# Expert 0's first window of rows moved into the attention's plan, expert 2's weight loads ordered behind transposes, and filler products in later gaps of TensorE

## The chip, the cores and the metric

The kernel runs on one core of one Trainium2 chip. The metric is the device time of one execution in microseconds (us). PE is TensorE, DVE is VectorE, ACT is ScalarE, POOL is GpSimd and SP is SyncE, whose only work here is to issue DMAs.

## The reference

Three stages follow one another, all in float32.

```
# 1. attention: 4 x 8 heads, 768 steps, head width 48
k_n = k / (norm(k) + 1e-06)
for t in range(S):
    y[:, :, t] = einsum('bhd,bhde->bhe', q[:, :, t], state)
    v_old = einsum('bhde,bhd->bhe', state, kt)
    state = state + bt * einsum('bhd,bhe->bhde', kt, vt - v_old)
x = y as 3072 rows of 384

# 2. routed layer: 8 experts, 384 -> 1024 -> 384; each row goes to the expert of its largest logit
e_idx = argmax(x @ w_gate)
h = max(x[mask] @ w1[e], 0); ye = h @ w2[e]
out[mask] = gate_w[mask] * eom[mask, e] * ye

# 3. dense layer: 4 experts, 384 -> 1024 -> 384, all rows through all of them
p = domain_probs / (sum(domain_probs) + 1e-09)
out += p[:, e] * (max(x @ w1[e], 0) @ w2[e])
```

Which rows an expert of stage 2 gets is known only from the attention's output.

## The kernel before

Each stage builds a `Plan` (L103): a list of operations with an engine, an assumed cost, what each reads and writes, and a priority (a lower number goes first). `order` (L130) schedules the list once, before the program is built, and the program then holds every engine's instructions in that fixed order. Nothing is reordered on the chip: an instruction that waits holds up everything behind it on its engine, and a DMA that waits holds up everything behind it on its queue.

**Attention.** The 768 steps go in 12 chunks of 64, each a chain of small matmuls with evacuations by ACT and DVE between them (`rw`, `Sp` and `pb` are its PSUM banks). As soon as a tile of 128 rows of output is there, `Router.done` transposes it (L529), copies it with ACT (`xT`), and multiplies it with the gate weights (L536), and `place` (L540 on) works out where each row goes (L554, L570). The last chunk's rows come out at the end, so that the last stretch is one chain: output, transpose, gate product, place, list of rows (`wid`, L615). Where the plan has a gap of more than 300 ns on PE, it puts `fill` in (L249): a 128 x 128 product on a tile of zeros into a bank's unused part, between `FROM` and `FEND` of planned time.

**Routed layer, `moe1`.** Weights are in two float16 parts (high and low, cast by ACT L738 and DVE L739), so are the rows (`xh`) and the hidden values (`h`), and each product takes three matmuls. An expert's rows are gathered by POOL (`xg<-xd,wid`, L774), normalised and split (DVE L578 to L583, ACT L581), transposed by a DMA of the SP queue (`xt<-xh`) and put through `window_` (L779): 72 matmuls with the first weight (L787), whose 8 results are evacuated by ACT (L789) and DVE (L790), and 72 with the second (L799), whose 3 results are evacuated by L801 and L802 and written to DRAM by the POOL queue (`x<-y`, L805). An expert has 432 rows at most in the fixed program. The first 192 rows of experts 0 and 1 are taken out of the first 16 tiles, gathered during the attention and transposed into `xe` (`early`, L584), and the weights of these two experts are cast during the attention (into `kq`, `wa` and `wb`). So experts 0 and 1 have an early window of 192 rows (`xe`) and a second one of 240 (`xt`); the others have one of 432. Weights of expert 2 go into `w`, those of expert 3 into `kq` again, those of expert 4 into `wa`. Weights pass through three staging tiles `s0` to `s2`.

The tiles of `moe1` are taken from the memory that the attention's tiles held; the framework adds the waits which that needs.

**Dense layer, `moe2`.** It reads the DRAM tiles `x2` block by block (L928, L947).

Of the kernel before, what the change touches and what calls it, by code (L numbers as in the profile page):

```python
# [17 lines left out]
N, DM, NE, FF, NE2 = 3072, 384, 8, 1024, 4  # L18
# [5 lines left out]
WIN = 432  # L24
# [65 lines left out]
TRI = 450  # L90
UP = 1070
PW = 1080
FEND = 100000
FIN = 6
GRP = (6, 6, 4, 6, 2)

# [386 lines left out]
class Router:  # L483

    NXR=4
    def __init__(self,ctx,tc,dp):
        self.tc=tc; self.nc=tc.nc; self.xd=dp.tile([N,XW],F32,name="xd"); self.eld=dp.tile([N+512,MW],F32,name="eld"); self.ord=dp.tile([NE*N+512,1],I32,name="ord")
        c=self.c=ctx.enter_context(tc.tile_pool(name="rc",bufs=1)); T=lambda n,s,d=F32: c.tile(s,d,name=n)
        self.wgo=T("wgo",[128,KD,16])
        self.tri=T("tri",[128,128],F16); self.ones16=T("ones16",[128,128],F16)  # L490
        self.desc=T("desc",[128,8])
        self.row=T("row",[128,NT,MW]); self.LG,self.pr,self.tok=self.row[:,:,0:16],self.row[:,:,16:20],self.row[:,:,20]; self.acc,self.wid=T("acc",[128,NE,4]),T("wid",[128,NE,4],U32); self.OH=T("OH",[128,NT,8],F16)
        self.M2,self.MX=(T(n,[128,NT]) for n in ("M2","MX")); self.RK=T("RK",[128,NT],I32); self.EL=T("EL",[128,4,4,MW]); self.am,self.sc=T("am",[128,4]),T("sc",[128,4])
        self.run=T("run",[128,8],F16); self.kq=T("kq",[128,2*KD*FF*2],F16); self.wa,self.wb=(T(n,[128,2*KD*FF],F16) for n in ("wa","wb")); self.cnt=T("cnt",[128,8])
        self.xe=[T(f"xe{e}",[128,2*KD,EW],F16) for e in range(2)]; self.few=T("few",[128,8])
# [215 lines left out]
class Moe:  # L711
# [3 lines left out]
    def __init__(self,ctx,tc,r,w1,w2,v1,v2,out):  # L715
        self.ctx=ctx; self.tc=tc; self.nc=tc.nc; self.r=r; self.w=(w1,w2); self.v=(v1,v2); self.out=out
        p=ctx.enter_context(tc.tile_pool(name="vw",bufs=1)); self.dp=ctx.enter_context(tc.tile_pool(name="mdp",bufs=1,space=DRAM))
        r.c=ctx.enter_context(tc.tile_pool(name="fin",bufs=1))
        n=2*KD*FF; self.kq=[r.kq[:,0:n],r.kq[:,n:]]
        self.vw=[[p.tile([128,2,KD,FF],F16,name=f"v1{e}") for e in range(2)],[p.tile([128,2,4,7,192],F16,name="v20")]]  # L720

        a=[t.bitcast(F32).rearrange("p (j d) -> p j d",d=DM) for t in (r.kq,r.wa)]; self.acc=lambda j: a[j//16][:,j%16]
        w=r.wb; self.xk=[[w[:,1024*(KD*i+k):1024*(KD*i+k)+1024].rearrange("p (y t) -> p y t",y=2) for k in range(KD)] for i in range(2)]
        self.x2=[self.dp.tile([128,2,N+WIN],F16,name=f"x2{k}") for k in range(KD)]
        pp=ctx.enter_context(tc.tile_pool(name="pp",bufs=1,space=PSUM)); self.bank=[pp.tile([128,512],F32,name=f"b{i}") for i in range(8)]
    gate=(); slow=1.0
    def op(self,e,dur,fn,reads=(),writes=(),**k):
        k.setdefault('prio',self.prio); self.pl.add(e,dur,fn,reads,writes,**k)
    def dma(self,out,in_,reads,writes,xfer,turn=False):
# [12 lines left out]
    def weight(self,t,key,src,n,width):  # L742

        t=t.rearrange("p (l n f) -> p l n f",l=2,n=n); step=1024//width
        v=src.rearrange("(n p) f -> p n f",p=128); self.claim(key)
        for a in range(0,n,step):
            m=step*width; s,k=self.stage(m)
            self.dma(s.rearrange("p (n f) -> p n f",f=width),v[:,a:a+step],(),[k],m*WX)
            h,l=(t[:,j,a:a+step].rearrange("p n f -> p (n f)") for j in range(2))
            for x in range(0,m,m//2): self.pair(s[:,x:x+m//2],h[:,x:x+m//2],l[:,x:x+m//2],[k,key],key+(a,x))  # L750
        out=[key+(a,x,j) for a in range(0,n,step) for x in (0,m//2) for j in (0,1)]; self.parts.setdefault(key,set()).update(out); return out
# [94 lines left out]
    def moe1(self):  # L846
        nc=self.nc; tc=self.tc; r=self.r; pl=self.pl=Plan(tc,HOP); self.si=self.xi=self.bi=self.ci=self.hi=self.yi=0; self.pp_=0; self.parts={}
        with ExitStack() as c:
# [7 lines left out]
            def fetch(e):  # L856
                if e>=NE: return
                i=B_[e]; self.prio=10*(e-1)-3; x=self.gather(wid[:,e],e,0 if e>1 else EW); self.prio=10*(e-2)+3 if e>2 else 2
                t=[t.rearrange("p (l n f) -> p l n f",l=2,n=n) for t,n in zip(W[i],(KD,KF))]
                kw=[self.weight(W[i][j],('W',i,j),self.w[j][e],n,f) for j,n,f in ((0,KD,FF),(1,KF,DM))] if e>1 else [[('W',i,0)],[('W',i,1)]]  # L860
                ahead[e]=x,t,kw
            def colf(e):
# [8 lines left out]
            for e in range(NE):  # L871
                x,t,kw=ahead.pop(e); self.prio=10*e+5
                for m in range(6):
                    if e==4: self.weight6(self.vw[0][0],('v',0,0),self.v[0][0],m)
                    if e==5 and m<4: self.weight7(self.vw[1][0],('v',0,1),self.v[1][0],m)
                    if e==6: self.weight6(self.vw[0][1],('v',1,0),self.v[0][1],m)
                if e==0:
                    colf(1); cols[0][0]=0; x1,t1,kw1=ahead[1]
                    self.pp_=0; self.window_(0,*t,kw,(r.xe[0],[]),cols[0]); self.pp_=3; late=self.window_(1,*t1,kw1,(r.xe[1],[]),cols[1],ys=ye)
                    self.pp_=6; put(0); self.window_(0,*t,kw,x,cols[0],EW); self.prio=10  # L880
                    for f in late: f()
                else:
# [105 lines left out]
def deltanet_moe(tc,q,k,v,beta,wg,wo,w1,w2,probs,v1,v2,out):  # L988
    nc=tc.nc
    with ExitStack() as ctx:  # L990
        dp=ctx.enter_context(tc.tile_pool(name="dp",bufs=1,space=DRAM))
        r=Router(ctx,tc,dp)
        with ExitStack() as c2:
            plan=Plan(tc,HOP)
            at=Attention(c2,tc,plan,q,k,v,beta,r.wa,r.wb,r.done)
            at.prio=0
            at.ahead=r.weights; r.setup(c2,at,plan,wg,wo,probs); r.ahead=(w1,w2); at.run(); r.counts()
            plan.emit()
        m=Moe(ctx,tc,r,w1,w2,v1,v2,out)
        m.moe1(); m.moe2()  # L1000
# [28 lines left out]
```

## Time and profile before

| | |
|---|---|
| runs (us) | 1251.54, 1254.93, 1254.89, median 1254.89 |
| profiled execution (us) | 1257.36 |
| its span (us) | 1255.8 |
| PE busy | 1179.4 us, 94% of the span |
| DVE, ACT, POOL busy | 62%, 49%, 51% |
| mean granted PE clock | 0.965 |

The profile covers one execution, and its times are counted from the span's start. The granted clock is 1.00 where PE runs at its higher level (2.4 GHz) all the time and 0.50 where it runs at the lower one (1.2 GHz). The attention ends at 311 us, the routed layer at 538 us, and the rest is the dense layer.

### The profile page before, as it was taken

Reading aid. Unit: us, or ns where it says so; the run is one execution under the profiler, and the core shown is the slowest. Engines: PE = TensorE matmul, PEld = TensorE weight load, DVE = VectorE, ACT = ScalarE, POOL = GpSimd, SP = SyncE. Lnnn points to the kernel's source line nnn. Section 1 sums busy time; section 2 is a strip of 40 time slices with the busy share of each in tenths; the row PEclk is TensorE's granted clock in tenths of the full one; section 3 lists DMA queues with packets and bytes.
Section 4 is the critical chain, followed back from the end, with each engine's and each line's share of the span. In section 5 each row is a group of like instructions: output and inputs, shape, how many; then the busy total and the mean of one; then the engine's idle time right before and its main releaser. Section 6 shows DMA issues by size and latency. Waiting matters only on the chain.

```text
span 1255.8 us, 38782 instructions
## 1 busy us (share of the span) xinstructions
PE 1179.4 (94%) x16595; PEld 1031.4 (82%) x16595; DVE 781.1 (62%) x1583; ACT 618.7 (49%) x1129; POOL 640.4 (51%) x896
## 2 busy tenths in 40 slices
PE   6988888877989999999999999999999999999997
PEld 5877777766974555589999999999999999999997
DVE  3766837664777787236666566677565776555555
ACT  4546664543545655235445444454444454444442
POOL 9643431442474350055665454576444675566565
PEclk9889998886999999999999999999999999999999
DMA  8445442324779976021111111111111220111101
GB/s 137 84 94 121 97 98 45 98 74 110 182 176 233 244 184 175 29 67 39 40 39 39 35 43 44 48 51 39 34 44 50 65 64 28 37 54 52 52 27 39
DMA packets 151457, 100.74 MB, mean 80 GB/s; under 512 B 107696, under 2 KB 140432, under 8 KB 151280
## 3 DMA queue, kind: packets, MB, share of 16 engines
q1 hardware_dynamic: 133520, 69.18, 22.4%
q0 software_dynamic: 9216, 23.50, 6.7%
q10 hardware_dynamic: 8544, 5.53, 1.5%
q8 instruction: 131, 2.15, 0.7%
q14 instruction: 46, 0.38, 0.1%
HBM read 77.09 MB, written 15.77 MB: 74 GB/s over the span
## 4 chain that ended last, share of the span: by engine, by line
PE 56%; DVE 0%; issue 0%; POOL 0%; ACT 0%; POOLq 0%
PE b L928 30%; PE b L947 26%; POOL out_dram L966 0%; DVE h L940 0%; DVE cc L958 0%; DVE wa L962 0%; DVE sm L958 0%; ACT h L939 0%; ACT a L930 0%; POOL sep L965 0%; POOLq L1024 0%; POOLq L966 0%
## 5 line engine op out<-in xcount | busy, mean ns | idle before, releaser
L928 PE MATMUL b<-wb,v 128*128 128x256 f16 x3456 | 392.6, 273 | 0.4 <-PEq L895 0.4
L928 PEld LDWEIGHTS <-v 128*128 128x128 f16 x3456 | 336.7, 98 | 37.8 <-issue 0.8
L947 PE MATMUL b<-v,h 128*128 128x192 f16 x4032 | 348.2, 246 | 0.0
L947 PEld LDWEIGHTS <-h 128*128 128x128 f16 x4032 | 335.5, 98 | 2.4 <-DVE h L940 0.2
L936 POOL TENSOR_TENSOR S<-a 128x256 f32<-128x256 f32 x192 | 150.8, 804 | 249.8 <-ACT a L930 249.5
L940 DVE TENSOR_TENSOR h<-a,h 128x768 f16<-128x768 f32 x96 | 132.6, 1381 | 134.8 <-ACT h L939 126.5
L940 DVE TENSOR_TENSOR h<-S,h 128x1024 f16<-128x1024 f32 x96 | 117.7, 1226 | 125.8 <-ACT h L939 125.6
L930 ACT ACTIVATE a<-b 128x512 f32<-128x512 f32 x192 | 113.8, 595 | 151.2 <-PE b L928 149.1
L939 ACT ACTIVATE h<-S 128x1024 f16<-128x1024 f32 x96 | 101.4, 1056 | 161.7 <-POOL S L936 142.1
L936 POOL TENSOR_TENSOR S<-S,a 128x256 f32<-128x256 f32 x96 | 126.9, 1322 | 0.0
L939 ACT ACTIVATE h<-a 128x768 f16<-128x768 f32 x96 | 80.9, 843 | 3.0
L936 POOL TENSOR_TENSOR S<-a,S 128x256 f32<-128x256 f32 x96 | 77.0, 802 | 7.2
L958 DVE TENSOR_TENSOR cc<-b,sm 128x192 f32<-128x192 f32 x192 | 58.5, 345 | 2.4 <-ACT sm L952 2.4
L789 ACT ACTIVATE h<-b 128x432 f16<-128x432 f32 (+2 forms) x80 | 35.7, 454 | 40.3 <-PE b L787 36.3
L805 POOL DMA_DIRECT2D x<-y x27 | 19.3, 721 | 68.9 <-DVE y L802 60.8
L790 DVE SCALAR_TENSOR_TENSOR h<-b,h 128x432 f16<-128x432 f32 (+2 forms) x80 | 40.7, 511 | 17.5 <-ACT h L789 17.1
L774 POOL DMA_INDIRECT xg<-xd,wid x28 | 30.2, 1077 | 38.7 <-DVE xh L583 22.0
L958 DVE TENSOR_TENSOR sm<-b,sm 128x192 f32<-128x192 f32 x144 | 46.2, 348 | 1.5
L799 PE MATMUL b<-h,kq 128*128 128x432 f16 (+2 forms) x288 | 42.4, 304 | 4.8 <-DVE h L790 4.8
L787 PE MATMUL b<-xt,w 128*128 128x432 f16 x216 | 42.1, 355 | 2.5 <-DVE wa L739 2.0
L739 DVE SCALAR_TENSOR_TENSOR v<-s,v 128x512 f16<-128x512 f32 (+2 forms) x56 | 41.6, 761 | 4.1 <-ACT v L738 3.9
L267 POOL DMA_DIRECT2D stw<-in_moe_w_dram x28 | 16.0, 571 | 52.6 <-DVE X L374 19.9
(279 smaller groups left out, 1748.0 us busy)
## 6 DMA issues: line engine op xcount, KB each, us to landing
wb<-x SPq DMA_DIRECT2D x72, 256.0 KB, 3.2
s<-in_moe_w_dram SPq DMA_DIRECT2D x40, 384.0 KB, 4.2
s<-in_moe_w_dram SPq DMA_DIRECT2D x18, 512.0 KB, 4.3
s<-in_moe_w_dram SPq DMA_DIRECT2D x24, 256.0 KB, 4.7
xd<-ys ACTq DMA_DIRECT2D x24, 192.0 KB, 3.1
x<-y POOLq DMA_DIRECT2D x18, 216.0 KB, 4.2
stw<-in_moe_w_dram POOLq DMA_DIRECT2D x12, 256.0 KB, 4.0
stw<-in_moe_w_dram POOLq DMA_DIRECT2D x16, 192.0 KB, 3.5
```

The costliest lines, as they stand in the source:

```text
L739: self.op('V',(150+1.042*n)*self.slow,lambda: self.nc.vector.scalar_tensor_tensor(out=lo,in0=s,scalar=64.0,in1=hi,op0=ALU.mult,op1=ALU.sub ...
L787: nc.tensor.matmul(out=ps,lhsT=w1[:,a,k,f*128:(f+1)*128],rhs=xt[:,b*KD+k],start=i==0,stop=i==8); i+=1
L789: self.op('A',160+.85*n,lambda ps=ps,h=h: nc.scalar.activation(out=h[:,0],in_=ps,func=AF.Relu),[('p1',pi)],[('h',hi,0)],**U)
L790: self.op('V',150+1.042*n,lambda ps=ps,h=h: nc.vector.scalar_tensor_tensor(out=h[:,1],in0=ps,scalar=0.0,in1=h[:,0],op0=ALU.max,op1=ALU.sub ...
L799: nc.tensor.matmul(out=ps,lhsT=w2[:,a,f,d*128:(d+1)*128],rhs=hs[f][0][:,b],start=(f,i)==(0,0),stop=(f,i)==(KF-1,2))
L928: for c,y in PASS: nc.tensor.matmul(out=F[k][:,f],lhsT=w[:,c,d,c_:c_+128],rhs=self.xk[B%2][d][:,y,256*i:256*i+256],start=(f,z)==(0,0),stop ...
L930: self.op('A',620,lambda k=k,g=g: A.activation(out=a[ja][:,g].rearrange("p x t -> p (x t)"),in_=F[k].rearrange("p a t -> p (a t)"),func=AF ...
L936: self.op('G',930,lambda o=o,x=x,y=y,w=w: G.tensor_tensor(out=X[o],in0=X[x],in1=X[y],op=w),ka,[ks])
L939: self.op('A',200+.833*m,lambda h=h,q=q,g=g: A.activation(out=h[:,0,:,q],in_=g,func=AF.Copy),kg,[kh+(0,)])
L940: self.op('V',1400 if m==768 else 1350,lambda h=h,q=q,g=g: V.tensor_tensor(out=h[:,1,:,q],in0=g,in1=h[:,0,:,q],op=ALU.subtract),kg+[kh+(0, ...
L947: for z,(c,d) in enumerate(PASS): nc.tensor.matmul(out=Q[k][:,o,0:192],lhsT=h[:,c,g,x],rhs=w[:,d,m,y],start=(m,o,z)==(0,0,0),stop=(m,z)==( ...
L958: self.op('V',340,lambda o=o,k=k,y=y,x=x: V.tensor_tensor(out=o,in0=Q[k][:,y,0:192],in1=s[:,x],op=ALU.add),[(qk,k),('sm',z,x)],[ko])
```

## The change

Three things are changed. Line numbers grow by 2 behind the constants and by 30 in the later part.

First, expert 0's early window (72 + 72 matmuls of 192 columns, 11 evacuations by ACT and 11 by DVE, three DMAs of the POOL queue) is built by a new `Router.window` into the attention's plan, with priority 20, which is behind everything of the attention itself. Its hidden values and results lie in `GQ3x` and `GQ41`, tiles that the attention is done with by then. It is taken out of `moe1`.

Second, `late` makes the loads of expert 2's weights depend, in the plan, on the key `('xt',0,0)`; when they are planned the last writer of that key is expert 2's own first transpose into `xt0`.

Third, `FEND` goes from 100000 to 400000, so that fillers may stand in gaps behind 100 us of planned time too. By the order of instructions there are 366 fillers where there were 252. The new ones stand in 12 runs: three in the middle of the attention (x2, x1, x12), the others in the stretch that is at 262 to 285 us before, in front of gate products (x12, x12), between two placements (x13), in front of the last chunk's L396 products (x7, x13, x17), behind L587 (x5), and in front of L410 products (x12, x8).

```diff
+EPR = 20
+LTK = ('xt', 0, 0)
...
-FEND = 100000
+FEND = 400000
...
+    def window(self,e):
...
+        at=self.at; nc=self.nc; n=EW; t=f"ew {e}"; at.prio=EPR+0.1*e; ...
+        U=[x.rearrange("p h i -> p (h i)").bitcast(F16)[:,2*n*j:2*n*j+2*n].rearrange("p (a t) -> p a t",a=2) for i in (3,4) for x in at.GQ[i] for j in range(5)]; ...
+        for f in range(KF):
...
+            at.op('P',9*(n/2.4+3),mm,kx+kw[0],[k],t,take=[k],lat=LP,ni=18)
+            at.op('A',160+.85*n,lambda P=P,h=h: nc.scalar.activation(out=h[:,0],in_=P[:,0:n],func=AF.Relu),[k],[kh+(0,)],t,after=free(s0+f))
...
+        for d in range(KD):
...
+                at.op('P',6*(n/2.4+3),mm,[('eh',e,f,j) for f in (f0,f0+1) for j in range(2)]+kw[1],[k],t,take=[k] if f0==0 else (),lat=LP,ni=12)
...
+            at.dma(self.x2[d][:,:,0:n],y,[ky+(0,),ky+(1,)],[('x2',d)],t,xfer=n*2,q='G')
...
-            self.dma(s.rearrange("p (n f) -> p n f",f=width),v[:,a:a+step],(),[k],m*WX)
+            self.dma(s.rearrange("p (n f) -> p n f",f=width),v[:,a:a+step],self.late,[k],m*WX)
...
+                t=[t.rearrange("p (l n f) -> p l n f",l=2,n=n) for t,n in zip(W[i],(KD,KF))]; self.late=[LTK] if e==2 else ()
...
-                    self.pp_=0; self.window_(0,*t,kw,(r.xe[0],[]),cols[0]); self.pp_=3; late=self.window_(1,*t1,kw1,(r.xe[1],[]),cols[1],ys=ye)
+                    self.pp_=3; late=self.window_(1,*t1,kw1,(r.xe[1],[]),cols[1],ys=ye)
...
-            at.ahead=r.weights; r.setup(c2,at,plan,wg,wo,probs); r.ahead=(w1,w2); at.run(); r.counts()
+            at.ahead=r.weights; r.setup(c2,at,plan,wg,wo,probs); r.ahead=(w1,w2); at.run(); r.window(0); r.counts()
```

Three places in the order of instructions follow. The first is the SP queue from the attention's last DMAs (`xd<-row`) on. Before, in its order:

```order
L267 DMA xd_57<-row_67 128x6x24
L732 DMA s0_5763<-in_moe_w1_dram 128x1024
L732 DMA s1_5764<-in_moe_w1_dram 128x1024
L732 DMA s2_5765<-in_moe_w1_dram 128x1024
L267 DMA xd_57<-row_67 128x2x24
L732 DMA s0_5763<-in_moe_w2_dram 128x2x384
L732 DMA s1_5764<-in_moe_w2_dram 128x2x384
L732 DMA s2_5765<-in_moe_w2_dram 128x2x384
L732 DMA_TRANSPOSE xt0_5742<-xh_5745 128x6x128
L732 DMA_TRANSPOSE xt0_5742<-xh_5745 128x6x112
```

Now, at the same place:

```order
L269 DMA xd_57<-row_70 128x6x24
L269 DMA xd_57<-row_70 128x2x24
L760 DMA_TRANSPOSE xt0_6025<-xh_6028 128x6x128
L760 DMA_TRANSPOSE xt0_6025<-xh_6028 128x6x112
L760 DMA_TRANSPOSE xt1_6026<-xh_6028 128x6x128
L760 DMA_TRANSPOSE xt1_6026<-xh_6028 128x6x112
L760 DMA_TRANSPOSE xt0_6025<-xh_6028 128x6x128 x2
L760 DMA s0_6046<-in_moe_w1_dram 128x1024
L760 DMA s1_6047<-in_moe_w1_dram 128x1024
L760 DMA s2_6048<-in_moe_w1_dram 128x1024
```

The six loads of expert 2's weights that stood ahead of the first transposes now stand behind six of them: two each for the second windows of experts 0 and 1 and two of expert 2.

The second place is ACT at the attention's end (`GQ<-pb` are evacuations of expert 0's window, `xT` those of the last router tiles, `h<-b` is the first of `moe1`). Now, from the third last router tile's end on:

```order
L257 ACTIVATE xT<-pb_151 128x384 [waits PE_49]
L626 ACTIVATE GQ_114<-pb_152 128x192 [waits PE_49]
L626 ACTIVATE GQ_114<-pb_150 128x192 [waits DVE_49,PE_49]
L626 ACTIVATE GQ_115<-pb_152 128x192 [waits PE_49,Pool_49]
L257 ACTIVATE xT<-pb_153 128x384 [waits DVE_49,PE_49,Activation_49]
L626 ACTIVATE GQ_115<-pb_151 128x192 [waits DVE_49,PE_49]
L626 ACTIVATE GQ_115<-pb_150 128x192 [waits PE_49]
L635 ACTIVATE GQ_117<-pb_151 128x192 [waits PE_49,Pool_49]
L635 ACTIVATE GQ_117<-pb_153 128x192 [waits DVE_49,PE_49]
L635 ACTIVATE GQ_117<-pb_152 128x192 [waits DVE_49,PE_49]
L817 ACTIVATE h_6029<-b_6012 128x192 [waits DMAHW0_49,DMASW6_49,DMAHW1_49,DMASW5_49,DMAHW3_49,DMASW4_49,DMAHW4_49,DVE_49,DMAHW5_49,PE_49,Pool_49]
```

Where two evacuations `xT` and then those of `moe1` stood, eight of expert 0's window stand between and behind them, and the first of `moe1` has three more waits, `DMASW4` to `DMASW6`, which are DMAs of the POOL queue.

The third place is POOL there (`x<-GQ` are the writes of expert 0's results, `ha` belongs to the last placement, `xg<-xd,wid` is the first gather of `moe1`). Before, in its order:

```order
L565 TENSOR_TENSOR he<-OH,oa_161 128x64 [waits DVE_49,Pool_49]
L567 TENSOR_TENSOR ha<-he,iv 128x2x32 [waits PE_49,Pool_49]
L567 TENSOR_TENSOR ha<-he,iv 128x2x32 [waits PE_49]
L774 DMA xg<-xd,wid 128x408 [waits DMAHW2_49,DMAHW3_49,DMAHW1_49,DMAHW4_49,DMAHW0_49,DMAHW5_49,DMASW6_49,DMAHW6_49,DMASW0_49,DMAHW7_49,DVE_49,Activation_49]
L774 DMA xg<-xd,wid 112x408
```

Now:

```order
L269 DMA x_59<-GQ_117 256x1x192 [waits DVE_49]
L567 TENSOR_TENSOR he<-OH,oa_164 128x64 [waits DVE_49,Pool_49]
L569 TENSOR_TENSOR ha<-he,iv 128x2x32 [waits PE_49,Pool_49]
L569 TENSOR_TENSOR ha<-he,iv 128x2x32 [waits PE_49]
L269 DMA x_60<-GQ_117 256x1x192 [waits DVE_49]
L269 DMA x_61<-GQ_117 256x1x192 [waits DMASW6_49,DVE_49]
L802 DMA xg<-xd,wid 128x408 [waits DMAHW2_49,DMAHW1_49,DMAHW3_49,DMAHW0_49,DMAHW4_49,DMASW6_49,DMAHW5_49,DMASW5_49,DMAHW6_49,DMASW4_49,DMAHW7_49,DMASW0_49,PE_49]
L802 DMA xg<-xd,wid 112x408
```

The three writes stand ahead of the gather, and the gather waits for their queue semaphores (`DMASW4` to `DMASW6`) as well, since tiles of `moe1` lie where their source lay.

## Rows read from the trace of the kernel before

**Rows 1.** The page: its first line, and engines in the chain that ended last.

```profile
span 1255.8 us, 38782 instructions
...
PE 56%; DVE 0%; issue 0%; POOL 0%; ACT 0%; POOLq 0%
```

**Rows 2.** Stretches: length, busy (x) of PE, PEld, DVE, ACT, POOL; PEclk, DMA share, GB/s.

```profile
300.00:310.00 10.00, 6.48 (x87) 5.10 (x85) 5.69 (x32) 1.47 (x3) 2.73 (x7) 0.50 0.55 177
310.00:320.00 10.00, 9.00 (x92) 8.80 (x92) 5.96 (x23) 4.40 (x12) 5.14 (x12) 0.78 0.40 117
...
340.00:350.00 10.00, 6.78 (x70) 6.38 (x68) 2.40 (x11) 5.05 (x13) 2.69 (x3) 1.00 0.50 116
...
380.00:390.00 10.00, 7.75 (x33) 3.46 (x32) 7.07 (x15) 4.69 (x11) 3.75 (x6) 0.83 0.93 209
```

**Rows 3.** PE in order of time, 289 to 312 us: start, duration, work, idle before.

```profile
289.07 1.54 PE L410 MATMUL rw<-Sf,kqT 112*64 112x96 f32 x32 [0.81 <-ACT Sf L255]
...
297.49 3.65 PE L410 MATMUL pb<-w,GQ 64*64 64x48 f32 x64
...
308.67 0.17 PE L554 MATMUL pb<-OH,tri 128*128 128x16 f16 x1 [1.28 <-DVE OH L551]
...
310.63 0.52 PE L570 MATMUL pb<-ha,hb 128*128 128x32 f16 x4 [0.62 <-POOL ha L567]
```

**Rows 4.** PE in order of time, one chunk earlier, and one filler group.

```profile
198.85 1.10 PE L410 MATMUL pb<-w,GQ 64*64 64x48 f32 x32
...
L250 PE MATMUL Sp<-wz 128*128 128x128 f16 x249 | 18.6, 232 | 0.0
```

**Rows 5.** PE in order of time, 311 to 405 us.

```profile
311.43 7.54 PE L787 MATMUL b<-xe,kq 128*128 128x192 f16 x72 [0.28 <-DVE acc L573]
...
332.65 2.00 PE L787 MATMUL b<-xt,kq 128*128 128x240 f16 x18 [0.81 <-DMA xt<-xh]
...
339.31 2.14 PE L799 MATMUL b<-h,wb 128*128 128x192 f16 x24
341.29 3.85 PE L787 MATMUL b<-xt,kq 128*128 128x240 f16 x36
344.98 1.80 PE L799 MATMUL b<-h,kq 128*128 128x240 f16 x16
351.13 0.47 PE L799 MATMUL b<-h,kq 128*128 128x240 f16 x3 [4.35 <-DVE h L790]
...
373.95 5.09 PE L787 MATMUL b<-xt,w 128*128 128x432 f16 x27
...
385.12 6.86 PE L787 MATMUL b<-xt,w 128*128 128x432 f16 x27 [1.98 <-DVE wa L739]
```

**Rows 6.** DVE in order of time, 311 to 351 us.

```profile
311.41 0.18 DVE L615 CAST wid<-acc 128x32 uint32<-128x32 f32 x1
...
325.83 0.61 DVE L583 SCALAR_TENSOR_TENSOR xh<-xg,sc,xh 112x384 f16<-112x384 f32 x1
...
350.54 0.23 DVE L208 TENSOR_TENSOR r<-ovt,kw 128x64 f32<-128x64 f32 x1 [6.68 <-POOL ovt L208]
...
351.10 0.61 DVE L583 SCALAR_TENSOR_TENSOR xh<-xg,sc,xh 128x384 f16<-128x384 f32 x1
```

**Rows 7.** DVE's groups of 311 to 332 us: count, busy us, mean ns, idle before.

```profile
L739 DVE SCALAR_TENSOR_TENSOR w<-s,w 128x512 f16<-128x512 f32 (+1 forms) x12 | 7.1, 616 | 0.2 <-ACT w L738 0.2
```

**Rows 8.** POOL in order of time, 313 to 347 us.

```profile
313.33 1.00 POOL L774 DMA_INDIRECT xg<-xd,wid  x1 [2.47 <-issue]
...
346.71 0.79 POOL L867 DMA_DIRECT2D eld<-EL  x1 [7.43 <-issue]
```

**Rows 9.** DMA issues: count, size, median us from issue to landing.

```profile
s<-in_moe_w_dram SPq DMA_DIRECT2D x40, 384.0 KB, 4.2
...
x<-y POOLq DMA_DIRECT2D x3, 96.0 KB, 3.9
```

**Rows 10.** PE's waits of 100 to 311 us: total us, times, longest.

```profile
PE rw L410 <- issue: 13.8, 12, 2.2
```

More of the change, by code (lines that the diff above doesn't have):

```diff
@@ L486, in __init__ @@
     def __init__(self,ctx,tc,dp):
-        self.tc=tc; self.nc=tc.nc; self.xd=dp.tile([N,XW],F32,name="xd"); self.eld=dp.tile([N+512,MW],F32,name="eld"); self.ord=dp.tile([NE*N+512,1],I32,name="ord")
+        self.tc=tc; self.nc=tc.nc; self.xd=dp.tile([N,XW],F32,name="xd"); self.eld=dp.tile([N+512,MW],F32,name="eld"); self.x2=[dp.tile([128,2,N+WIN],F16,name=f"x2{k}") for k in range(KD)]; self.ord=dp.tile([NE*N+512,1],I32,name="ord")
         c=self.c=ctx.enter_context(tc.tile_pool(name="rc",bufs=1)); T=lambda n,s,d=F32: c.tile(s,d,name=n)
@@ L609, in weights, with lo, mm @@
                     at.op(WLE,70+1.042*m,lambda s=s,h_=h_,l_=l_: nc.vector.scalar_tensor_tensor(out=l_,in0=s,scalar=64.0,in1=h_,op0=ALU.mult,op1=ALU.subtract),ks+k,[('W2',e,w,a,x)],g)
+    def window(self,e):
+        at=self.at; nc=self.nc; n=EW; t=f"ew {e}"; at.prio=EPR+0.1*e; w=[x.rearrange("p (l n f) -> p l n f",l=2,n=m) for x,m in zip(((self.kq[:,0:2*KD*FF],self.kq[:,2*KD*FF:]),(self.wa,self.wb))[e],(KD,KF))]
+        kw=[[(z,e,0,a,x) for z in ('W','W2') for a in range(KD) for x in range(0,FF,512)],[(z,e,1,a,0) for z in ('W','W2') for a in range(KF)]]
+        U=[x.rearrange("p h i -> p (h i)").bitcast(F16)[:,2*n*j:2*n*j+2*n].rearrange("p (a t) -> p a t",a=2) for i in (3,4) for x in at.GQ[i] for j in range(5)]; free=lambda s: [('GQ',3+s//10,hh,s//5%2) for hh in range(2)]
+        hs=U[0:8] if e==0 else U[8:16]; y0=16; s0=8*e; x=self.xe[e]; kx=[('xe',e,j) for j in range(2)]
+        def lo(q,k,o,reads,wr,give,op0,sc): at.op('V',150+1.042*n,lambda: nc.vector.scalar_tensor_tensor(out=o[:,1],in0=q(),scalar=sc,in1=o[:,0],op0=op0,op1=ALU.subtract),reads,wr,t,give=give)
+        for f in range(KF):
+            k=('ep',e,f); P=Lazy(at,k); h=hs[f]; kh=('eh',e,f)
+            def mm(P=P,f=f):
+                i=0
+                for d in range(KD):
+                    for a,b in ((0,0),(0,1),(1,0)): nc.tensor.matmul(out=P[:,0:n],lhsT=w[0][:,a,d,f*128:f*128+128],rhs=x[:,b*KD+d],start=i==0,stop=i==8); i+=1
+            at.op('P',9*(n/2.4+3),mm,kx+kw[0],[k],t,take=[k],lat=LP,ni=18)
+            at.op('A',160+.85*n,lambda P=P,h=h: nc.scalar.activation(out=h[:,0],in_=P[:,0:n],func=AF.Relu),[k],[kh+(0,)],t,after=free(s0+f))
+            lo(lambda P=P: P[:,0:n],k,h,[k,kh+(0,)],[kh+(1,)],[k],ALU.max,0.0)
+        for d in range(KD):
+            k=('eq',e,d); P=Lazy(at,k); y=U[y0+d]; ky=('ey',e,d)
+            for f0 in range(0,KF,2):
+                def mm(P=P,d=d,f0=f0):
+                    for f in (f0,f0+1):
+                        for i,(a,b) in enumerate(((0,0),(0,1),(1,0))): nc.tensor.matmul(out=P[:,0:n],lhsT=w[1][:,a,f,d*128:d*128+128],rhs=hs[f][:,b],start=(f,i)==(0,0),stop=(f,i)==(KF-1,2))
+                at.op('P',6*(n/2.4+3),mm,[('eh',e,f,j) for f in (f0,f0+1) for j in range(2)]+kw[1],[k],t,take=[k] if f0==0 else (),lat=LP,ni=12)
+            at.op('A',160+.85*n,lambda P=P,y=y: nc.scalar.activation(out=y[:,0],in_=P[:,0:n],func=AF.Copy,scale=2.0**-8),[k],[ky+(0,)],t,after=free(y0+d))
+            lo(lambda P=P: P[:,0:n],k,y,[k,ky+(0,)],[ky+(1,)],[k],ALU.mult,2.0**-8)
+            at.dma(self.x2[d][:,:,0:n],y,[ky+(0,),ky+(1,)],[('x2',d)],t,xfer=n*2,q='G')
@@ L723, in __init__ @@
         w=r.wb; self.xk=[[w[:,1024*(KD*i+k):1024*(KD*i+k)+1024].rearrange("p (y t) -> p y t",y=2) for k in range(KD)] for i in range(2)]
-        self.x2=[self.dp.tile([128,2,N+WIN],F16,name=f"x2{k}") for k in range(KD)]
+        self.x2=r.x2
         pp=ctx.enter_context(tc.tile_pool(name="pp",bufs=1,space=PSUM)); self.bank=[pp.tile([128,512],F32,name=f"b{i}") for i in range(8)]
-    gate=(); slow=1.0
+    gate=(); slow=1.0; late=()
     def op(self,e,dur,fn,reads=(),writes=(),**k):
@@ L858, in fetch @@
                 i=B_[e]; self.prio=10*(e-1)-3; x=self.gather(wid[:,e],e,0 if e>1 else EW); self.prio=10*(e-2)+3 if e>2 else 2
-                t=[t.rearrange("p (l n f) -> p l n f",l=2,n=n) for t,n in zip(W[i],(KD,KF))]
+                t=[t.rearrange("p (l n f) -> p l n f",l=2,n=n) for t,n in zip(W[i],(KD,KF))]; self.late=[LTK] if e==2 else ()
                 kw=[self.weight(W[i][j],('W',i,j),self.w[j][e],n,f) for j,n,f in ((0,KD,FF),(1,KF,DM))] if e>1 else [[('W',i,0)],[('W',i,1)]]
```

## The prediction

> **What bounds the kernel now.** The first view is the page. Its chain of waits is PE for 56% [rows 1]; that is the dense layer, which follows the routed layer and runs on PE without gaps. The change leaves the dense layer alone, so whatever the routed layer ends earlier or later is what the time changes by. The second view is the busy time by stretches of 10 us [rows 2]. At the attention's end, 300 to 310 us, PE is busy for 6.48 us at a granted clock of 0.50, its lower level; from 310 to 320 it gets 0.78. Later holes are at 340 to 350 (6.78 us busy) and 380 to 390 (7.75 us at 0.83). The third view is PE in order of time [rows 3, 5]: the tail is a chain of small products waiting for DVE and POOL (1.28 and 0.62 us), one run of 64 products takes 3.65 us there, and `moe1` starts at 311.43 us. Expert 0's second window starts at 332.65, released by the transpose; a stall of 4.35 us ends at 351.13; expert 2 starts at 373.95; a stall of 1.98 us ends at 385.12. So there is room for PE work in the tail, and there are about 6.3 us of later stalls that a shifted schedule may lose or keep.
>
> **The change, part by part.**
>
> *Expert 0's window, its PE work.* It is 144 matmuls. 24 of the same shape take from 339.31 to 341.29, 1.98 us [rows 5], so 144 take 11.9 us. From the last chunk's start at 289.07 to `moe1`'s at 311.43 are 22.4 us [rows 3, 5]. Of these PE idles 3.5 us in 300 to 310 [rows 2], 0.6 before the last placement and 0.3 before `moe1` [rows 3, 5]: 4.4 us. The lower clock costs there: the run of 64 took 3.65 us, and 32 of it took 1.10 at the full level [rows 3, 4], so 1.5 us; of the other 5.4 busy us of 300 to 310 at clock 0.50 [rows 2], half would be 2.7, and I take 2, since part is latency of short runs. With expert 0's matmuls in the gaps the tail needs 22.4 - 4.4 - 3.5 + 11.9 = 26.4 us and ends at 315.5. I take T0, the last evacuation of expert 0, at 315 with the fillers' half us below. Bounds: 313.5 if the smaller gaps before 300 fill too, 318 if blocks of 18 matmuls (1.5 us each) stand ahead of chain links that were ready. So expert 0's 11.9 us, and the 1.7 us or so that its first matmuls lost at the lower clock (72 took 7.54 us [rows 5], at 0.0825 they are 5.9), cost 3.6 us of the tail instead of 13.6.
>
> *What follows T0.* The order shows the catch: the first gather of `moe1` and the first evacuation by ACT wait for the landing of expert 0's three writes, because the new tiles lie where the results lay. Before, the gather ran at 313.33, 1.9 us behind the row list at 311.41 [rows 6, 8]. Now the last write must be issued (0.7 us, the length of such an issue being 0.79 at most in [rows 8]) and land; writes of this very size took 3.9 us [rows 9]. So the gather starts near 315 + 0.7 + 3.9 + 0.4 = 320, 6.7 us later than before. Behind ACT stand all evacuations: PE can do 27 matmuls of expert 1 (three banks, 2.2 us), then idles about 3 us and may restart at the lower level.
>
> The Trainium skill, "DMA: Bandwidth & Descriptors", section "Anatomy of one DMA — SWDGE (gpsimd) path", fits a POOL-queue DMA by 2.0 us plus bytes by 436e3 per us, mostly the receipt of the write, which for 96 KB is an estimate of 2.2 us. By it the gather would start 1.7 us earlier and the time would be 1247.7; the trace's 3.9 us disagrees, and I use the trace.
>
> From the gather to expert 0's second window it was 332.65 - 313.33 = 19.3 us [rows 5, 8]. There DVE also cast weights of expert 2, 12 casts of 0.62 us, 7.1 us [rows 7], which now come later; so normalisation comes some 3 us sooner behind the gather, and with the 6.2 us from the last `xh` (ended 326.44) to the window [rows 5, 6] it starts at about 335.5. Nothing else is left by then, so PE stands before it and restarts at the lower clock, 1.6 us as for expert 0's first run. Before, 60 matmuls of expert 1's early window were still to be done behind 332.65 (the last 24 of them are in [rows 5]), 5.0 us.
>
> *Experts 0 and 1, second windows.* They are 288 matmuls of 240 columns; 36 take from 341.29 to 344.98 [rows 5], 0.1025 each, so 29.5 us. Before, PE needed 373.95 - 332.65 = 41.3 us up to expert 2: 5.0 + 29.5, the stall of 4.35, and 2.4 of smaller ones and of a restart at the lower clock. That stall came because a DVE instruction of the overflow lists (`r<-ovt`) waited 6.68 us [rows 6] for POOL, whose second `eld` write waited 7.43 us [rows 8], and an evacuation stood behind it. In the new order it stands behind expert 0's last hidden values, so PE, which has 72 further matmuls to do with these, does not see it. What is late behind it now is expert 2's weights.
>
> *Expert 2's weights.* Their first loads leave the start of the queue and stand behind six transposes. The `xh` of the fifth and sixth stand on DVE right behind `r<-ovt`, as before, when the one ended at 351.7 [rows 6]. With POOL's waits as they were it is about 351 again, so the loads go out at 352 to 354 and land 4.2 us later [rows 9], at 357. The casts are planned between the evacuations of expert 1's second window, so that behind the first cast five of eight evacuations wait for that landing; PE, with three banks, stands for an estimated 3 us (bounds 0, if the transposes come by 348, and 8, the whole of the 6.68 us wait and what follows). The six casts of the first weight then end near 366, those of the second near 375, at the 12 in 14.5 us of before. Expert 2 starts at 335.5 + 1.6 + 29.5 + 3 = 369.6, 4.4 before 373.95, and needs its second weight 13 us later. It fits with some 4 to 7 us to spare; without that cover it is a rival below.
>
> *The stall at 385.12* and its lower clock (27 matmuls in 6.86 instead of 5.09 us [rows 5]) are worth 3.8; half of that, 1.9, is my gain, bounds 0 and 3.8. Later casts, which all come by some 25 us behind their old places, take 0.8 of it back.
>
> *Fillers.* 114 more. A filler takes 18.6/249 = 0.075 us [rows 4], 8.5 us in all, in gaps. Below: each that finds no gap delays PE by as much, at worst some 1.5 us where gaps turn out shorter. Above: one more run like that of 64 brought to the full level gives 1.5 us. I take a gain of 0.5.
> PE's sequencer also stalls on "issue", 13.8 us in 12 places from 100 to 311 us [rows 10], and fillers add 228 instructions to its stream. The Trainium skill, "Runtime: NRT & Kernel Launch", section "Instruction fetch mechanics", says that crossing a block of 256 instructions is mostly hidden; by it the additions cost nothing. The stalls in the trace do not look hidden; a further block would cost at most the longest, 2.2 us, and this is inside the range.
>
> *Sum.* 4.4 at expert 2's start (the fillers are in T0), 1.9 at the stall, less 0.8: 5.5 us. The profiled execution took 1257.36 us (span 1255.8 [rows 1]), so 1251.9 for its like; the median of the runs is 2.5 lower, so **1249.4 us**.
>
> **The rivals.** A measurement of this kernel tells some 0.3%, 3.8 us, from no change.
>
> - *The landing is hidden.* If the writes land while PE still has work, or the tail ends early, the 3.1 us of waiting and the slow restart (1.6) do not show, and expert 1's 3 us go too: 5.5 + 7.7 = 13.2 us, 1241.7, of which I take 12. Against it: the order lets PE do 2.2 us only. Chance 0.12.
> - *The landing eats it.* The window moves, but the stalls only change places: expert 1 waits 6 us instead of 3 for the casts and the stall at 385.12 stays, gain 0 to 2, about 1254. For it: POOL's second `eld` write waits for the first wherever it stands. Chance 0.29. This is also how it looks if the change does not do what it says.
> - *Slower: expert 2's weights.* The SP queue is in order. If T0 is 318 and the gathers of expert 1, whose `eld` write all hangs on, come 4 us later than I have them, the loads go out near 360, the first weight is cast at 373, expert 2 starts behind 376, its second weight comes at 383 to 388, and expert 3's, which share the staging tiles, follow: 4 to 9 us lost, 1261. It decides when the first load is issued behind 358. For it: DVE was busy for 7.07 of 10 us from 380 to 390 with weights that were ahead [rows 2], so a late start is caught up slowly. Against it: DVE has less to do before 350. Chance 0.19.
>
> **How the numbers follow.** The forecast (4 to 8.5 us gained) has the remaining 0.40, 1246.5 to 1251 being its own range. Faster by over 0.3%: 0.40 and 0.12, 0.52. Within: 0.29. Slower: 0.19. The range goes from 1242, the hidden landing, to 1258.5, which leaves out the worse half of the slower case and what lies beyond a complete gain: 1242 to 1258.5.
>
> **What would show it.** In the changed profile: PE at 297 to 311 us at a granted clock near 1.00 with expert 0's L624 between the router's products; last evacuation at about 315; ACT and POOL idle for some 4 us behind it, then the first gather at about 320; expert 0's second window at about 335.5; no PE wait for `r<-ovt`; the first load of expert 2 at 352 to 354; expert 2 at 367 to 371. I am wrong if the tail still runs at 0.50 (T0 at 318 or later), if the gather starts before 318 or behind 322, if the first load goes out behind 358, or if PE waits for a weight cast (L767) of expert 2 or 3.

## The result, and the profile after

The changed kernel took 1240.05 us in the median (1236.2 to 1240.45, 4 runs) beside 1253.22 for the kernel before (1250.63 to 1254.93, 4 runs): a ratio of 0.989, 95% interval 0.9861 to 0.9919, 13.2 us less. The forecast was 1249.4 with a range down to 1242: the sign is right, the size is 2.4 times the one forecast, and the time lies below the range. In two later groups of runs, each on one chip, the changed kernel's ratio was 0.9897 (0.9861 to 0.9933) and 0.9894 (0.9856 to 0.9931).

The two profiled executions are 21 us apart, more than the medians: repeated executions of one kernel spread here by some 10 us (the kernel before took 1241.51 to 1256.25 in 17 runs on one chip), and the profiled execution before, 1257.36 us, is slower than every other one recorded of its kernel. Part of the 21 us arises before the change can act: the first full run of L396 (L398 in the changed kernel) starts at 54.78 us before and at 50.68 after. So executions are compared below by times counted from the end of the row list's instruction (`wid`), and verdicts rest on the ratios.

The page's first line, and the stretches of [rows 2]:

```profile
span 1234.6 us, 38985 instructions
```

```profile
300.00:310.00 10.00, 9.24 (x132) 9.11 (x132) 4.67 (x25) 1.32 (x4) 4.04 (x8) 1.00 0.13 34
310.00:320.00 10.00, 7.48 (x84) 6.74 (x82) 5.16 (x25) 2.82 (x10) 5.39 (x14) 1.00 0.30 83
...
340.00:350.00 10.00, 9.65 (x95) 9.05 (x94) 6.89 (x18) 6.13 (x15) 7.67 (x14) 1.00 1.05 280
...
380.00:390.00 10.00, 9.69 (x54) 5.03 (x53) 7.71 (x20) 6.02 (x12) 4.98 (x6) 1.00 1.03 252
```

PE is busy for 9.24 us of the tail's 10 at the full clock, where it was 6.48 at half, and the holes at 340 and 380 are gone. A new one is at 310 to 330 (7.48 and 7.16 us busy). PE in order of time, for [rows 3, 5]:

```profile
291.59 2.07 PE L412 MATMUL pb<-w,GQ 64*64 64x48 f32 x64
...
306.80 0.25 PE L572 MATMUL pb<-ha,hb 128*128 128x32 f16 x4
307.82 2.40 PE L815 MATMUL b<-xe,wa 128*128 128x192 f16 x27 [0.76 <-DVE GQ L618]
311.77 3.87 PE L815 MATMUL b<-xe,wa 128*128 128x192 f16 x45 [1.55 <-DVE h L818]
...
325.97 7.55 PE L815 MATMUL b<-xt,kq 128*128 128x240 f16 x72 [2.84 <-DMA xt<-xh]
...
356.01 13.30 PE L815 MATMUL b<-xt,w 128*128 128x432 f16 x72
...
382.29 5.09 PE L815 MATMUL b<-xt,kq 128*128 128x432 f16 x27
```

The 27 matmuls of expert 1 that the order allowed are there, then the wait for the landing. DVE and POOL, for [rows 6, 8]:

```profile
307.32 0.18 DVE L643 CAST wid<-acc 128x32 uint32<-128x32 f32 x1
307.41 0.35 DVE L618 SCALAR_TENSOR_TENSOR GQ<-pb,GQ 128x192 f16<-128x192 f32 x1
310.61 0.06 DVE L210 MEMSET off<- 128x1 f32 x1 [2.85 <-DMA x<-GQ]
...
336.08 0.23 DVE L210 TENSOR_TENSOR r<-ovt,kw 128x64 f32<-128x64 f32 x1 [1.71 <-issue]
```

```profile
308.06 0.68 POOL L269 DMA_DIRECT2D x<-GQ  x1 [0.58 <-DVE GQ L618]
311.23 1.04 POOL L802 DMA_INDIRECT xg<-xd,wid  x1 [2.48 <-PE b L815]
...
316.14 0.21 POOL L584 COPY EL<-xg 128x21 f32<-128x21 f32 x1
...
332.24 0.81 POOL L895 DMA_DIRECT2D eld<-EL  x1 [4.04 <-DVE h L818]
```

The last write is issued at 308.06 and releases DVE at 310.61, 2.55 us later. Expert 2's loads go out at 339.73:

```profile
320.79 18.89 SPq L760 DMA_TRANSPOSE xt<-xh  x6
339.73 1.54 SPq L760 DMA_DIRECT2D s<-in_moe_w_dram  x3
```

### The profile page after: what moved, and what is told of

The parts are those of the page before. It is cut to its first block, busy times and chain, and to the rows that moved or that the text cites. A ratio compares the mean times of both kernels' runs of the same rounds, so it can differ in the third digit from the quotient of the medians.

```text
span 1234.6 us, 38985 instructions
## 1 busy us (share of the span) xinstructions
PE 1169.5 (95%) x16709; PEld 1024.0 (83%) x16709; DVE 780.1 (63%) x1583; ACT 619.5 (50%) x1129; POOL 641.8 (52%) x896
## 4 chain that ended last, share of the span: by engine, by line
PE 76%; DMA 9%; DVE 5%; issue 5%; ACT 2%; POOL 1%; SPq 1%; DVEq 0%; ACTq 0%; POOLq 0%
PE b L956 29%; PE b L975 26%; PE b L815 3%; PE rw L412 3%; DMA x<-y 3%; PE b L827 3%; PE pb L412 2%; DMA s<-in_moe_w_dram 2%; PE pb L398 2%; DMA kf<-in_k_dram 2%; PE pb L341 2%; PE pb L326 2%; DMA xt<-xh 1%; PE Sp L412 1%; PE pb L538 1%
## 5 line engine op out<-in xcount | busy, mean ns | idle before, releaser
L818 DVE SCALAR_TENSOR_TENSOR h<-b,h 128x432 f16<-128x432 f32 (+2 forms) x72 | 37.9, 527 | 17.3 <-ACT h L817 17.1
L817 ACT ACTIVATE h<-b 128x432 f16<-128x432 f32 (+2 forms) x72 | 32.8, 465 | 29.8 <-PE b L815 29.2
L815 PE MATMUL b<-xt,w 128*128 128x432 f16 x216 | 40.1, 346 | 0.3 <-DVE h L818 0.3
L260 POOL TENSOR_TENSOR v<-v,nt 128x384 f32<-128x384 f32 x24 | 20.5, 864 | 37.5 <-DMA v<-in_v_dram 15.2
```

The source lines that it names most:

```text
L815: nc.tensor.matmul(out=ps,lhsT=w1[:,a,k,f*128:(f+1)*128],rhs=xt[:,b*KD+k],start=i==0,stop=i==8); i+=1
L818: self.op('V',150+1.042*n,lambda ps=ps,h=h: nc.vector.scalar_tensor_tensor(out=h[:,1],in0=ps,scalar=0.0,in1=h[:,0],op0=ALU.max,op1=ALU.sub ...
```

## The experiments

Sixteen runs were made in four groups of four, of the changed kernel (twice) and of eleven others, three of them twice; each group shares a chip and its runs of the kernel before. A ratio belongs to all runs of a kernel and is not that of the medians. The table gives for one profiled execution of each kernel the start of a piece of work behind the end of the row list's instruction: the first gather, expert 0's second window (L787 or L815 on `xt,kq`), expert 2, and the dense layer. Each is read from the rows in order of time, for the change for instance 325.97 - 307.50 = 18.5.

| kernel | ratio, 95% interval | gather | 2nd window | expert 2 | dense |
|---|---|---|---|---|---|
| before | | 1.7 | 21.1 | 62.4 | 226.2 |
| changed | 0.989 (0.9861 to 0.9919) | 3.7 | 18.5 | 48.5 | 208.8 |
| changed, again | 0.9897 (0.9861 to 0.9933) | 3.7 | 16.6 | 46.7 | 205.5 |
| changed, third | 0.9894 (0.9856 to 0.9931) | 3.7 | 18.3 | 50.5 | 210.5 |
| fillers alone | 0.9999 (0.9975 to 1.0023) | 0.8 | 18.9 | 59.8 | 217.8 |
| window alone | 0.9979 (0.9949 to 1.0009) | 3.7 | 22.2 | 55.4 | 219.4 |
| window, fillers | 0.9991 (0.9970 to 1.0011) | 3.7 | 22.1 | 55.9 | 218.6 |
| order of loads alone | 0.9962 (0.9934 to 0.9989) | 0.8 | 20.6 | 57.0 | 216.6 |
| window, order | 0.9884 (0.9851 to 0.9916) | 3.7 | 16.8 | 49.4 | 207.4 |
| changed, only 2nd weight behind | 0.9963 (0.9946 to 0.9980) | 3.7 | 22.1 | 55.0 | 214.5 |
| changed, early loads, late casts | 0.9914 (0.9883 to 0.9945) | 3.7 | 20.4 | 51.7 | 211.9 |

Single executions differ by several us (the dense layer starts at 205.5 to 210.5 in three of the changed kernel), and the row of the kernel before is that of its 1257.36 us. So differences of rows in the table do not add up to the ratios.

**Fillers alone.** The kernel before with one line changed:

```diff
-FEND = 100000
+FEND = 400000
```

> The kernel before with the fillers of the change alone (FEND 400000). Theory: the fillers hold the granted clock at 1.00 from 255 us to the attention's end, so chains of small products run at the full level; the last row list comes 5 to 6 us earlier than in the kernel before, and with the old stalls of the routed layer kept the time is 1247 to 1249. Rival: the whole gain is expert 0's window, whose matmuls raise the clock themselves; then this kernel takes 1253, as before.

It took 1246.62 us beside 1246.93: nothing, though the granted clock did rise (1.00 in 260 to 280, 0.83 before). My theory, formed from the profile pair, fell. The kernel without them, FEND at 100000 in the changed code:

> The change without its fillers (FEND 100000). Theory: loses the 5 to 6 us that the fillers gave before 290 us, 1245 to 1247. Rival: expert 0's matmuls hold the clock by themselves, 1240 to 1241.

It took 1233.68 beside 1246.93, the whole gain. Its clock by stretches:

```profile
260.00:270.00 10.00, 6.67 (x167) 5.56 (x167) 5.89 (x16) 5.13 (x13) 5.92 (x13) 0.83 0.29 82
270.00:280.00 10.00, 5.30 (x313) 4.55 (x303) 6.15 (x15) 4.96 (x13) 4.46 (x6) 1.00 0.23 56
280.00:290.00 10.00, 9.61 (x250) 9.05 (x254) 3.84 (x9) 4.18 (x10) 1.19 (x2) 0.66 0.39 83
290.00:300.00 10.00, 9.87 (x325) 8.72 (x314) 4.28 (x16) 5.27 (x12) 1.17 (x2) 1.00 0.47 68
```

In two of the three stretches from 260 to 290 the clock is lower (0.83 and 0.66; the kernel before has 0.83 in all three, the changed kernel 1.00), without a loss that can be measured. From 290 on, where expert 0's matmuls stand and no fillers, it is 1.00. A run of the same code on a second chip gave 0.9894 (0.9871 to 0.9917), with this expectation:

> The change without its fillers again, beside the next run, which differs only in where expert 0's results lie. Theory: 1 to 4 us slower than the next. Rival (the landing is hidden): the same within 1 us.

**Without the ordering.** The changed kernel with expert 2's loads at the queue's head:

```diff
-self.late=[LTK] if e==2 else ()
+self.late=()
```

> The change without the ordering of expert 2's loads: they stand at the head of the queue again, ahead of the first transposes. Theory: the loads, which wait for the attention's tiles and for casts, hold up the transposes of expert 0, whose second window starts 2 to 4 us later, 1242 to 1244. Rival: the loads are out of the way by then and the weights come sooner, 1239 to 1240.

It took 1245.82 beside 1246.93. The loads cost not 2 to 4 us but the whole gain. The window alone, with FEND at 100000 as well:

> Expert 0's window in the attention's plan alone: no fillers behind 100 us, and expert 2's loads at the head of the queue. Theory: the window by itself gains nothing, because the queue's head keeps the transposes back; ratio to the kernel before 0.997 to 1.003. Rival: the run without the ordering was lowered by the fillers, and the window alone gains 4 us or more.

1245.58 beside 1249.15: the rival is not excluded at its lower end, but most of the gain is gone. And the ordering alone, in the kernel before:

> The kernel before with the ordering of expert 2's loads alone. Theory: the ordering is the cause and works without the window: transposes go out as soon as their rows are split, casts no longer stand among the early windows' evacuations, and 6 to 10 us are gained (ratio 0.992 to 0.995). Rival: the ordering pays only where the window has moved, since otherwise the casts of expert 2 come too late behind the longer early windows; ratio 0.998 to 1.004.

1241.81 beside 1249.15, a gain of some 5 us by the ratio (0.0038 x 1249), between theory and rival, and less than the 12 us ((0.9979 - 0.9884) x 1249) that it brings where the window has moved. Added up, the two alone would make 0.9941; the five runs that have both, with and without fillers, lie at 0.9884 to 0.9897. So they are worth more together, by a difference little larger than the intervals. PE's busy time in the 70 us behind the row list shows how (length; busy us of PE, PEld, DVE, ACT, POOL; clock). Window alone, ordering alone, and the changed kernel:

```profile
302.92:372.92 70.00, 58.30 (x508) 48.67 (x509) 51.53 (x148) 38.87 (x91) 42.10 (x86) 0.93 0.83 214
```

```profile
304.42:374.42 70.00, 68.79 (x645) 60.55 (x644) 46.21 (x142) 35.00 (x85) 41.28 (x89) 0.96 0.71 167
```

```profile
307.50:377.50 70.00, 63.98 (x550) 51.57 (x551) 49.28 (x147) 34.45 (x80) 43.11 (x91) 1.00 0.74 184
```

With the ordering alone PE idles for 1.2 of 70 us: it is bound by its own work, expert 0's window among it. With the window alone it idles for 11.7, in the changed kernel for 6.0: the work that moved away has left a hole, and the ordering closes half of it. Where the hole is, PE in order of time with the window alone:

```profile
307.19 3.87 PE L815 MATMUL b<-xe,wa 128*128 128x192 f16 x45 [1.54 <-DVE h L818]
...
325.14 9.90 PE L815 MATMUL b<-xt,kq 128*128 128x240 f16 x72 [8.14 <-DMA xt<-xh]
```

PE waits for expert 0's transposes for 8.14 us, against 2.84 in the changed kernel, and the next 72 matmuls take 9.90 us instead of 7.55, partly at the lower clock (0.75 in 325 to 335).

**What in the early loads costs it.** Two runs take them apart. In the first, of the loads only those of the second weight stand behind the transposes; the first weight's three are at the head:

```diff
-kw=[self.weight(...) for j,n,f in ((0,KD,FF),(1,KF,DM))]
+kw=[(setattr(self,'late',[LTK] if (e,j)==(2,1) else ()),self.weight(...))[1] for j,n,f in ((0,KD,FF),(1,KF,DM))]
```

> The change with the ordering only for expert 2's second weight: its first weight's three loads, which wait for no cast, are at the head of the queue again, the others stay behind the six transposes. Theory of the queue: transposes are held up by loads that wait for a staging tile to be cast, so the first three loads cost nothing, first transposes 11 to 13 us behind the row list, ratio 0.986 to 0.991 as for the change. Rival theory of the casts: what holds up the rows is DVE and ACT casting expert 2's weights ahead of the normalisation; six of the twelve casts are back, so the first transpose comes 13.5 to 15 us behind the list and the ratio is 0.992 to 0.996.

1244.09 beside 1248.75, ratio 0.9963; the first transpose came 16.2 us behind the row list. My theory of the queue fell: no load ahead of the transposes waited for a cast, and the loss stayed. The theory of the casts had the direction right and the size too small. In the second run the same three loads are early, too, but their casts are planned behind expert 2's first transpose:

```diff
-self.dma(...,self.late,[k],m*WX)
+self.dma(...,self.late if n==KF else (),[k],m*WX)
...
-self.pair(s[:,x:x+m//2],h[:,x:x+m//2],l[:,x:x+m//2],[k,key],key+(a,x))
+self.pair(s[:,x:x+m//2],h[:,x:x+m//2],l[:,x:x+m//2],[k,key]+list(self.late),key+(a,x))
```

> The change with the three loads of expert 2's first weight at the head of the queue, but the casts of them planned behind expert 2's first transpose. Theory: the casts are what costs; with the loads early and the casts late the gain is whole again, first transpose 11 to 13.5 us behind the row list, ratio 0.986 to 0.991. Rival: early loads cost by themselves (they share the DMA engines with the gathers and stand ahead of the transposes), ratio 0.994 to 0.998, as with loads and casts early.

1238.61 beside 1248.77, ratio 0.9914, and the first transpose at 14.6. The two runs differ in the place of the casts alone (on two chips, each beside its own runs of the kernel before), and their intervals do not overlap: the early casts are the larger part of the loss, some 6 us ((0.9963 - 0.9914) x 1249). From there to the changed kernel on the same chip, 0.9894, is within the intervals, so what early loads cost by themselves is not shown in the time. The traces show it on the gathers. The first gather on POOL and the copy that its landing releases, with the window alone and then with early loads and late casts:

```profile
306.65 1.03 POOL L802 DMA_INDIRECT xg<-xd,wid  x1 [2.49 <-PE b L815]
...
314.39 0.20 POOL L584 COPY EL<-xg 128x21 f32<-128x21 f32 x1 [1.67 <-DMA xg<-xd,wid]
```

```profile
312.21 1.02 POOL L802 DMA_INDIRECT xg<-xd,wid  x1 [2.49 <-PE b L815]
...
319.91 0.20 POOL L584 COPY EL<-xg 128x21 f32<-128x21 f32 x1 [1.62 <-DMA xg<-xd,wid]
```

What the view of the gathered tile says of the six gathers up to 330 us, with the window alone and in the changed kernel's second run:

```profile
DMA to landing us min/median/max: 5.8/6.4/7.7
```

```profile
DMA to landing us min/median/max: 3.0/3.2/3.8
```

From gather to copy it is 7.7 us in both runs and 4.9 in the changed kernel (311.23 to 316.14), where the copy does not wait for the landing but stands behind POOL's three further gathers. So the loads cost 2.8 us there, casts or no casts. With the window alone the second window starts 3.7 us later than in the changed kernel (22.2 and 18.5). Besides these 2.8, another 1.8 are lost from the end of the second split to the window, on the way of the transposes (319.34 to 325.14, 5.8; 321.97 to 325.97, 4.0), and 0.9 are won between copy and split, where DVE in the changed kernel waits for ACT. The casts stand there; DVE with the window alone, and the splits with early loads and late casts:

```profile
314.83 0.69 DVE L767 SCALAR_TENSOR_TENSOR w<-s,w 128x512 f16<-128x512 f32 x1
...
316.75 0.68 DVE L767 SCALAR_TENSOR_TENSOR w<-s,w 128x512 f16<-128x512 f32 x1
...
317.46 0.62 DVE L585 SCALAR_TENSOR_TENSOR xh<-xg,sc,xh 128x384 f16<-128x384 f32 x1
...
318.73 0.61 DVE L585 SCALAR_TENSOR_TENSOR xh<-xg,sc,xh 112x384 f16<-112x384 f32 x1
```

```profile
322.46 1.15 DVE L585 SCALAR_TENSOR_TENSOR xh<-xg,sc,xh 128x384 f16<-128x384 f32 x2
```

From the copy to the end of the second split it is 4.95 us with early casts and 3.7 with late ones. In the table the two runs that differ in the casts alone are 1.7 us apart at the second window and 3.3 at expert 2; where the rest of the 6 us is lost was not traced.

**The wait for the landing.** Expert 0's results are put into the tile of its input, `xe0`, which no tile of the routed layer covers:

```diff
+U[16:19]=[x[:,2*d:2*d+2] for d in range(KD)]
...
-at.op('A',..., [k],[ky+(0,)],t,after=free(y0+d))
+at.op('A',..., [k],[ky+(0,)],t,after=kx)
```

> The change with expert 0's results kept in the tile of its input, which the routed layer's tiles do not cover, so the first gather and the first evacuations do not wait for the three writes to land. Theory: the gather is released by the row list and starts 2 us sooner (1.9 us behind the list), and since expert 0's second window hangs on it, the time falls by 2 us, to 1238. Rival: what follows waits for weights or for the overflow lists anyway, 1240.

1233.23 beside 1246.93, ratio 0.9879 (0.9848 to 0.9910). Again, beside the changed kernel on one chip, and the reference itself:

> The change with expert 0's results in the tile of its input, fillers kept, beside the changed kernel. Theory: 2 to 4 us under it. Rival: equal within 1 us.

> The changed kernel again, for the run before it. Every theory: ratio 0.988 to 0.991.

1236.9 and 1235.74, ratios 0.9907 (0.9878 to 0.9937) and 0.9894: by this pair nothing is gained. The gather did start 0.8 us behind the row list instead of 3.7, and expert 0's second window at 15.4 instead of 18.3, but expert 2 at 50.7 instead of 50.5. What is gained is given back here:

```profile
316.60 7.55 PE L815 MATMUL b<-xt,kq 128*128 128x240 f16 x72 [1.22 <-DMA xt<-xh]
...
338.66 1.08 PE L815 MATMUL b<-xt,wa 128*128 128x240 f16 x9 [3.43 <-DVE h L818]
```

PE stands for 3.43 us within expert 1's second window, for an evacuation that stands on DVE behind a split of rows:

```profile
337.68 0.61 DVE L585 SCALAR_TENSOR_TENSOR xh<-xg,sc,xh 48x384 f16<-48x384 f32 x1 [3.81 <-ACT xh L583]
338.21 0.39 DVE L818 SCALAR_TENSOR_TENSOR h<-b,h 128x240 f16<-128x240 f32 x1
```

ACT's part of that split had waited 3.81 us for a transpose. The stall has the size that I had forecast for the change, but not the cause: no cast stands ahead of it. The same without fillers, twice, the first time beside the changed kernel:

> The changed kernel itself again, as a reference on this chip. Every theory: ratio 0.986 to 0.992.

> The change without its fillers and with expert 0's results in the tile of its input, so that nothing waits for their writes. Theory: fillers are worth nothing and the wait for the landing 2 us; ratio 0.986 to 0.988, 2 us under the changed kernel. Rival: the landing is hidden, ratio equal to that of the changed kernel.

> The change without fillers and with expert 0's results in the tile of its input again. Theory: first gather 0.8 us behind the row list instead of 3.7, expert 2 starts 2 to 3 us sooner behind the list, ratio 0.984 to 0.988. Rival: the sooner start is given back at the weights, ratio 0.988 to 0.990.

1236.38 for the changed kernel, 1228.76 (0.9859, 0.9819 to 0.9900) and 1233.06 (0.9869, 0.9842 to 0.9896) without fillers and wait, the last beside 1235.92 for the kernel without fillers alone, whose expert 2 starts 2.2 us later behind the row list (49.9 and 47.7). These are the lowest ratios of all, yet every interval overlaps that of the kernel it should beat, so whether the wait costs 0 or 3 us stays open.

**Two more tries.** The loads behind four transposes instead of six (`LTK = ('xt', 1, 0)`), and early loads with late casts, both without fillers and wait:

> The kernel without fillers and with the results in the input's tile, the loads now behind four transposes instead of six. Theory: the transposes of experts 0 and 1 are what PE waits for, expert 2's own are not urgent; weights come some 8 us sooner and nothing is lost, ratio 0.984 to 0.988. Rival: casts fall among the second windows' evacuations and cost what they save elsewhere, ratio 0.988 to 0.992.

> The same, without fillers and with expert 0's results in the tile of its input. Theory: both savings add up, ratio 0.983 to 0.987. Rival: the weights are not what the second windows wait for, so early loads add nothing to the kernel without them, 0.985 to 0.988.

0.9908 (0.9885 to 0.9931) and 0.9892 (0.9852 to 0.9933): neither beats the plain version.

## Why the prediction was wrong in size

**The step that failed** is the one on expert 2's weights. In the sum, the new place of their loads comes to nothing: "normalisation comes some 3 us sooner behind the gather" gains 3, and "PE, with three banks, stands for an estimated 3 us" takes 3 back, so that the gain is left to the moved window and to half of a later stall. The runs showed the opposite: the window alone brings 0.9979, 3 us (at most 6), and the ordering beside it some 12. The estimated stall did not come. The second windows took 30.0 us (325.97 to 356.01) where I had 34.1 with it and a restart at the lower clock. The loads went out 32.0 us behind the last evacuation (307.76 to 339.73), not 37 to 39 (352 to 354, from 315), since `r<-ovt` waited 1.71 us, not 6.68 [rows 6]. Why POOL's second `eld` write ahead of it waited 4.04 us instead of 7.43 [rows 8] was not tested. And the prediction did not see that the early loads slow the gathers.

The other terms were nearer.

**The tail** is counted from the last run of 64 on `pb<-C,L`, before and after:

```profile
274.99 1.41 PE L396 MATMUL pb<-C,L 64*64 64x64 f32 x64 [1.43 <-DVE EL L579]
```

```profile
268.88 1.28 PE L398 MATMUL pb<-C,L 64*64 64x64 f32 x64
```

Up to `moe1` it took 36.4 us before (to 311.43), up to the last evacuation of expert 0 it takes 38.9 (to 307.76): 2.4 more, where I had 3.6. The half clock in [rows 2] is gone, and the run of 64 takes 2.07 us instead of 3.65 [rows 3].

**The landing** was mis-sized. I took 5.0 us from the last evacuation to the gather; it was 3.5 (307.76 to 311.23), since the write landed in 2.55 us, not in 3.9 [rows 9]. Here the estimate by the Trainium skill, "DMA: Bandwidth & Descriptors", section "Anatomy of one DMA — SWDGE (gpsimd) path" (2.2 us for 96 KB), was nearer than the median of the rows.

**From the gather to the second window** it was 14.7 us, where I had 15.5 (19.3 less 3, as the text has it, would be 16.3). PE did not restart at the lower clock in this execution: the 72 matmuls took 7.55 us, 0.1025 each. In the changed kernel's third run they took 8.89, so the 1.6 us of a restart are a matter of the execution.

In these four, 1.2 (tail) + 1.5 (landing) + 0.8 (to the second window) + 4.1 (the second windows) = 7.6 us less than forecast; with the 5.5 forecast, 13.1, and the medians say 13.2. That they agree so closely is in part luck, since each term comes from one execution of either kernel. The gather at 311.23 also lies outside the 318 to 322 that the prediction named, by the first two of these terms and by 6.1 us that arose ahead of the tail (274.99 and 268.88).

**The stall at 385.12**, for which the sum holds 1.9, was no term of the change. The kernel with fillers alone, whose routed layer is that of before, does not have it in its execution:

```profile
361.42 13.30 PE L787 MATMUL b<-xt,w 128*128 128x432 f16 x72
```

It takes 26.3 us from expert 2 to expert 3 as the changed one does; the profiled execution before took 31.0 (404.96 - 373.95). **The fillers** were sized at 0.5 and gave nothing measurable. Of the rivals, the one nearest is the first, the landing hidden, by its gain of 12 us; its reason was wrong, since the landing was not hidden, and taking the wait away brought between nothing and 3 us.

## What to carry to other kernels

Where work is moved off the busy engine, look at what that engine waits for next, here gathered rows, and clear that path too; each half alone brought 1 to 5 us by the ratios, both 13. A load that nobody needs soon is not free: its casts stand in order ahead of work that is needed now, and beside it the gathers landed later. Two single profiles differ by more than the change; count from a common event and let repeated runs judge.

## What the runs showed of the hardware

A gather landed in 3.0 to 3.8 us where no load was issued beside it (the changed kernel's second run) and in 5.8 to 7.7 where six loads of 384 to 512 KB were issued among the gathers (the window alone). And the lower clock in two stretches of 10 us of the attention (0.83 and 0.66 of full speed, in the kernel without the fillers) cost nothing measurable; that PE's small products wait there for the other engines would explain it and was not tested further.
